# Scan and maxout kernel: two up-projections over weight differences, the third folded into the output product

## The chip, the cores and the metric

One Trainium2 chip, one core. The metric is the device time of one execution in microseconds, median of the timed runs.

## The reference

```python
# part one: a chunked state-space scan over x (4, 8, 768, 32), a, B, C -> y, same shape as x
# bridge: y becomes 3072 tokens of 256 values
x = np.ascontiguousarray(attn_out.transpose(0, 2, 1, 3)).reshape(B * S, H * D)
# part two: w1, w2, w3 are 256 x 768, w_out is 768 x 256
h = np.maximum(np.maximum(x @ w1, x @ w2), x @ w3)
return (h @ w_out).astype(np.float32)
```

All inputs and the output are float32.

## The kernel before

The 768 positions of the sequence are cut into six blocks (`c` = 0 to 5) of 128 positions. A block holds all four batches, so 512 tokens. For each block the scan gives `yT[c]`, the 256 values by 512 tokens, transposed. The feed-forward part then makes up-projections a, b, c with w1, w2, w3, their maximum `h`, and the output product with w_out. The scan of block n = c + 1 is woven into the feed-forward part of block c.

Block 0 is computed with plain products (`whole_group`, 512 columns each) while weights still arrive. Blocks 1 to 5 use a scheme that multiplies 2 x 2 blocks with seven products in place of eight. A slot `k` is one weight matrix (index i) for one pair of the six 128-column pieces of the hidden size (index q): seven products of 128 x 128 by 256 columns. Before, a block has nine slots, k = 3q + i.

A slot has two halves. `early` issues four products into the PSUM tiles sumA (one buffer) and sumB (two buffers), a ScalarE copy (L653) and three VectorE adds (L654 to L656). `late` issues the other three products, into parts of the same banks that the adds have read, then the first quarter of the maximum (L667, a copy, for i = 0; L669 otherwise) and one add of 512 (L670). It returns the maximum over the other three quarters (L673, 768 wide), which is put at the head of the list `later`. `pop(n)` runs the next n entries of `later`, so it decides where they stand in VectorE's queue.

The operands of the seven products are blocks of the weights and of y and sums of them. `weight_sums(k)` makes the four sums of a slot's weights on GpSimd (L613 to L616), two slots ahead of their use in block 1; they serve for all later blocks. `scan_sums` makes the four of y on VectorE (L553).

`down_next` issues half of the output product of one group of 128 tokens: three of six 128 x 128 by 256 products, into a bank from `ffn_bank`, which has one buffer by then. Four calls fill a bank, ScalarE copies it to SBUF and SP's queue stores it. The output products of block c run during block c + 1; those of block 5 come after everything else and are stored from ScalarE's queue.

The scan's steps that lie in the slots: `transposed` (trB and trC, L410), `scores` (L483: eight products over four banks from `att_bank`, which then has four buffers in rotation; the four products of scores and decay mask, L491 on VectorE, go to `later`), `scan_state` (L451, the sum into the state, `scan_sum`, goes to `later`), and "y" (`scan_old`, `scan_own`: L506 and L519, then `scan_y` and `scan_sums`). The masks come from DRAM; `decay_masks` (L384) clears the upper half on GpSimd and `part` does the exponentials on ScalarE (L391), four at a call. Block c + 2 is loaded on SP's queue in slot 0.

No scheduler reorders anything: each engine runs its instructions in the order in which the program issues them. That order is written by hand: for each slot the tables X, Y, P, D and K say which scan step or output product stands between `early` and `late` or behind `late`, and how many entries of `later` are run where. "E" below is `early`, "L" is `late`, "D" is `down_next`.

Of the kernel before, what the change touches and what calls it, by code (L numbers as in the profile page):

```python
# [19 lines left out]
def kernel(  # L20
# [398 lines left out]
    def scan_c(c):  # L419

        st = blocks[c]
        tr = st["trC"]
        st["CT"] = CT = att.tile([HN, NB, 2, P], FP32, tag="CT", name="CT")
        for g in range(2):
            nc.scalar.mul(CT[:, :, g], tr, parity[:, g:g + 1])
# [98 lines left out]
    def first_own(bs):  # L524
# [9 lines left out]
        if 0 not in yT:  # L534
            yT[0] = ffn.tile([P, KD, BLK], FP32, tag="yT", name="yT")
# [4 lines left out]
    def scan_y(c):  # L540
        yT[c] = ffn.tile([P, KD, BLK], FP32, tag="yT", name="yT")
        for t in range(KD):
            nc.scalar.copy(out=yT[c][:, t], in_=blocks[c]["y"][t].rearrange("p b i -> p (b i)"))
# [45 lines left out]
    NW = 3 * NQ  # L589
# [17 lines left out]
    def weight_sums(k):  # L607
        q, i = divmod(k, 3)
        a11, a12, a21, a22 = (
            w_sb[i][:, kk, (2 * q + g) * P:(2 * q + g + 1) * P]  # L610
# [7 lines left out]
    def left(p, k):  # L618
        if p in (1, 2, 4):
            q, i = divmod(k, 3)  # L620
            g, row = {1: (0, 0), 2: (0, 1), 4: (1, 1)}[p]
            f = 2 * q + g
            return w_sb[i][:, row, f * P:(f + 1) * P]
# [17 lines left out]
    def early(c, k):  # L641
        q, i = divmod(k, 3)
# [5 lines left out]
        if i > 0 and k % 2 not in quarters:  # L648
            quarters[k % 2] = kilos(HB)[:, 0:3]
        t = held["m"][:, 1:4] if i == 0 else quarters[k % 2]  # L650
# [8 lines left out]
    def late(c, k):  # L659
        q, i = divmod(k, 3)  # L660
# [3 lines left out]
        to = h_of(c)[:, 2 * q:2 * q + 2].rearrange(  # L664
            "p g (r t) -> p (g r) t", r=2) if i == 2 else m
        if i == 0:
            nc.scalar.copy(out=m[:, 0], in_=A[:, 0])  # L667
        else:
            nc.vector.tensor_tensor(out=to[:, 0], in0=m[:, 0], in1=A[:, 0], op=ALU.max)  # L669
        nc.vector.tensor_tensor(  # L670
            out=t[:, 0:2], in0=B, in1=eu[:, 1:2].to_broadcast([P, 2, HB]), op=ALU.add)
        if i > 0:
            return [lambda: nc.vector.tensor_tensor(  # L673
                out=to[:, 1:4], in0=m[:, 1:4], in1=t, op=ALU.max)]
        return []

    downs = []

    def down_next(kind=ffn_bank):
# [5 lines left out]
        last = c == NC - 1  # L685
        if j % (2 if last else 4) == 0:
# [3 lines left out]
        for f in range(half * NQ, (half + 1) * NQ):  # L690
            nc.tensor.matmul(  # L691
                out=o[:, i], lhsT=hT[c][:, f, b * P:(b + 1) * P], rhs=wo_sb[:, f],
                start=(f == 0), stop=(f == NF - 1), skip_group_check=True)
        if last and j % 2:
            ob = ffn.tile([P, 2, DM], FP32, tag="ob", bufs=3, name="ob")[:, 0]
            nc.scalar.copy(out=ob, in_=o[:, i])
            nc.scalar.dma_start(
                out=out.rearrange("(b s) m -> s b m", s=S)[c * P:(c + 1) * P, b], in_=ob)
        if not last and j % 4 == 3:
# [4 lines left out]
                in_=ob)  # L704

# [97 lines left out]
    for n in range(NF * 3):  # L803
# [58 lines left out]
        if n == 17:  # L862
# [15 lines left out]
    X1 = ["tc", "D", "D", "s0", "D", "s2", "A", "y", "D"]  # L878
    Y1 = ["", "", "D", "", "", "D", "", "D", "D"]
    P1 = [(1, 0, 0), (1, 0, 0), (1, 0, 1), (1, 4, 1), (1, 0, 0), (1, 1, 3), (1, 1, 0), (1, 0, 0),  # L880
          (9, 0, 0)]
    D1 = [(0, 0), (1, 0), (2, 0), (2, 0), (2, 0), (1, 0), (0, 2), (0, 1), (0, 2)]
    K1 = {0: (0, (0, 1)), 2: (0, (2, 3)), 4: (1, (0, 1)), 6: (1, (2, 3))}
    X2 = ["t", "s0", "D", "s2", "D", "y", "D", "D", "D"]
    Y2 = ["D", "D", "D", "", "", "", "", "", ""]
    P2 = [(1, 0, 1), (1, 2, 2), (1, 0, 0), (1, 4, 1), (1, 0, 0), (1, 0, 0), (9, 0, 0), (1, 0, 0),
          (1, 0, 0)]
    D2 = [(0, 0), (1, 0), (1, 0), (1, 0)] + 5 * [(0, 1)]
    K2 = {3: (1, (0, 1)), 5: (1, (2, 3))}
    X3, Y3, P3 = 8 * ["D"] + [""], 9 * [""], 9 * [(1, 0, 0)]  # L890

    for c in range(1, NC):
        n = c + 1
        xs, ys, ps_, ds, ks = (
            (X1, Y1, P1, D1, K1) if c == 1 else (X2, Y2, P2, D2, K2) if n < NC else
            (X3, Y3, P3, D2, {}))
        for k in range(NW):
            early(c, k)
            if c == 1 and k < 2:
                sign()  # L900
                if k == 0:
                    decode()
            part(n, ds[k][0])
            part(n + 1, ds[k][1])
            pop(ps_[k][0])
            x = xs[k]
            if x == "D":
                down_next()
            elif x == "A":
                later.append(scan_state(n, att_bank))  # L910
            elif x == "tc":
                scan_tc(n, att_bank)
            elif x == "t":
                transposed(n)
            elif x == "s0":
                scores(n, 0)
            elif x == "s2":
                scores(n, 2)
                if 1 < c < NC - 2:
                    later.insert(2, scan_state(n, ffn_bank))  # L920
            elif x == "y":
                scan_old(n)
                scan_own(n, range(NB))
                scan_y(n)
                scan_sums(n)
            pop(ps_[k][1])
            maximum = late(c, k)
            if c == 1 and k + 2 < NW:
                weight_sums(k + 2)
            if n < NC and k == 0:  # L930
# [47 lines left out]
```

## Time and profile before

| | |
|---|---|
| median of 3 timed runs | 296.35 us (296.31 to 296.82) |
| profiled execution, span from first to last instruction | 300.1 us |
| TensorE (PE) busy | 287.4 us, 96% |
| VectorE (DVE) busy | 199.9 us, 67% |
| ScalarE (ACT) busy | 121.1 us, 40% |
| GpSimd (POOL) busy | 72.1 us, 24% |
| start of blocks 1, 2, 3, 4, 5 in the span | 64.9, 113.2, 158.2, 203.2, 247.9 us |

The profiled execution has no time of its own beside the span. Matmuls are pipelined and their ends are modelled, so the price of one is read from the starts of a long row of them. A float32 matmul of this kernel shows as two records; a transpose as one.

### The profile page before, as it was taken

The page shows a single profiled execution, that of the slowest core. Times are in us where ns is not written, and L with a number is a line of the kernel's source. Part 1 is how long each engine was busy: PE and PEld are TensorE (multiplying, and loading weights), DVE is VectorE, ACT ScalarE, POOL GpSimd, SP SyncE. Part 2 cuts the span into 40 slices and gives each one's busy share as a digit, 9 for nine tenths or more (in the row PEclk, how much of TensorE's full clock was granted, in tenths as well). Part 3 has the DMA queues.
Part 4 walks back from the last instruction along what each step waited for, and adds up shares of the span by engine and source line. Part 5 has one row for each costly group of instructions (what it writes and reads, how often), then busy time and mean ns, then how long its engine had stood idle before and what let it go on. Part 6 is the DMA issues. An engine that isn't in the chain of part 4 may idle for free.

```text
span 300.1 us, 5303 instructions
## 1 busy us (share of the span) xinstructions
PE 287.4 (96%) x2024; PEld 225.1 (75%) x2024; DVE 199.9 (67%) x382; ACT 121.1 (40%) x315; POOL 72.1 (24%) x96
## 2 busy tenths in 40 slices
PE   6679999999999999999999999999999999999995
PEld 4557435477677788888888888888887888888784
DVE  2752867989588556867676867676867676667540
ACT  2934687943672545334344334344330211011200
POOL 5241647468991600007000006000000000000000
PEclk9957999999999999999999999999999999999999
DMA  7989879969969105792007790001010001010101
GB/s 88 189 274 290 214 140 175 223 173 183 177 141 127 35 2 167 186 131 46 2 0 207 162 136 22 3 2 35 0 37 0 2 0 35 2 36 0 35 20 52
DMA packets 105049, 28.13 MB, mean 94 GB/s; under 512 B 75328, under 2 KB 101952, under 8 KB 105024
## 3 DMA queue, kind: packets, MB, share of 16 engines
q1 hardware_dynamic: 104144, 27.14, 45.6%
q10 hardware_dynamic: 880, 0.66, 0.7%
q8 instruction: 16, 0.26, 0.4%
q14 instruction: 9, 0.07, 0.1%
HBM read 24.54 MB, written 3.24 MB: 93 GB/s over the span
## 4 chain that ended last, share of the span: by engine, by line
PE 81%; DVE 7%; POOL 3%; DMA 3%; SPq 2%; issue 2%; ACT 1%; POOLq 0%; DVEq 0%; ACTq 0%
PE sumB L628 25%; PE o L691 19%; PE sumA L628 18%; PE up L578 5%; PE s L483 4%; DMA raw_x<-in_x_dram 3%; PE y L519 3%; DVE L L491 2%; PE up L570 2%; PE y L506 1%; POOL w_u L185 1%; PE y L530 1%; SPq L125 1%; PE A L451 1%; SPq L159 1%
## 5 line engine op out<-in xcount | busy, mean ns | idle before, releaser
L691 PE MATMUL o<-wo,h 128*128 128x256 f32 x288 | 68.9, 379 | 0.0
L691 PEld LDWEIGHTS o<-wo,h 128*128 128x128 f32 x288 | 54.7, 190 | 7.4
L628 PE MATMUL sumA<-yT,w 128*128 128x256 f32 x180 | 55.5, 390 | 0.4 <-DVE eu L654 0.3
L391 ACT ACTIVATE L<-L,ncums 128x128 f32<-128x128 f32 x160 | 50.3, 391 | 8.9 <-POOL L L384 8.9
L653 ACT COPY eu<-sumA 128x256 f32<-128x256 f32 x45 | 16.7, 372 | 89.2 <-PE sumA L628 80.6
L628 PE MATMUL sumB<-rb 128*128 128x256 f32 x180 | 46.2, 379 | 0.0
L654 DVE TENSOR_TENSOR eu<-sumA,eu 128x256 f32<-128x256 f32 x45 | 19.0, 422 | 31.1 <-ACT eu L653 31.1
L628 PEld LDWEIGHTS sumA<-yT,w 128*128 128x128 f32 x180 | 31.9, 189 | 9.4 <-issue 2.5
L628 PEld LDWEIGHTS sumB<-rb 128*128 128x128 f32 x180 | 34.2, 190 | 4.6
L491 DVE TENSOR_TENSOR L<-s,L 128x512 f32<-128x512 f32 x46 | 29.3, 680 | 3.1 <-PE s L483 2.7
L578 PE MATMUL up<-yT,w 128*128 128x512 f32 x64 | 29.1, 600 | 0.2 <-DVE w L188 0.2
L628 PE MATMUL sumB<-yT,rb 128*128 128x256 f32 x90 | 27.6, 389 | 1.6 <-DVE rb L656 1.3
L670 DVE TENSOR_TENSOR rb<-sumB,eu 128x512 f32<-128x512 f32 x30 | 20.7, 689 | 10.9 <-PE sumB L628 10.8
L628 PE MATMUL sumA<-rb 128*128 128x256 f32 x90 | 26.9, 380 | 0.3 <-DVE rb L553 0.3
L628 PE MATMUL sumB<-rb,w 128*128 128x256 f32 x90 | 26.8, 379 | 0.0
L185 POOL TENSOR_TENSOR w_u<-w_u,w_r 128x512 uint32<-128x512 uint32 x12 | 15.3, 1272 | 32.6 <-DVE w_u L179 19.0
L578 PEld LDWEIGHTS up<-yT,w 128*128 128x128 f32 x64 | 11.6, 190 | 14.7 <-issue 11.6
L655 DVE TENSOR_TENSOR v<-sumB,eu 128x256 f32<-128x256 f32 x45 | 19.1, 425 | 4.7
L384 POOL TENSOR_SCALAR_AFFINE_SELECT L<-L 128x1024 f32<-128x1024 f32 x20 | 22.2, 1138 | 0.0
L628 PEld LDWEIGHTS sumB<-yT,rb 128*128 128x128 f32 x90 | 16.1, 189 | 7.0 <-DVE rb L656 2.1
L628 PEld LDWEIGHTS sumA<-rb 128*128 128x128 f32 x90 | 17.0, 190 | 2.9 <-POOL rb L613 0.7
L628 PEld LDWEIGHTS sumB<-rb,w 128*128 128x128 f32 x90 | 17.1, 190 | 2.3
(101 smaller groups left out, 324.0 us busy)
## 6 DMA issues: line engine op xcount, KB each, us to landing
L<-cums SPq DMA_DIRECT2D x10, 1024.0 KB, 8.8
rb<-in_moe_w_dram SPq DMA_DIRECT2D x9, 512.0 KB, 7.4
raw_x<-in_x_dram SPq DMA_DIRECT2D x6, 512.0 KB, 7.8
out_dram<-ob SPq DMA_DIRECT2D x10, 256.0 KB, 2.3
raw_B<-in_B_dram SPq DMA_DIRECT2D x6, 256.0 KB, 4.9
raw_C<-in_C_dram SPq DMA_DIRECT2D x6, 256.0 KB, 6.3
rb<-in_moe_w_out_dram SPq DMA_DIRECT2D x3, 512.0 KB, 6.3
E<-cums SPq DMA_DIRECT2D x40, 32.0 KB, 3.8
```

Of the source, the lines that this page charges most:

```text
L185: nc.gpsimd.tensor_tensor(out=u, in0=u, in1=r, op=ALU.add)
L384: nc.gpsimd.affine_select(out=Ls[c][:, b], in_=Ls[c][:, b], pattern=[[0, NH], [1, P]], compare_op=ALU.is_ge, fill=MASKED, base=0, channel_ ...
L391: nc.scalar.activation(L[:, b, h], L[:, b, h], AF.Exp, bias=ncum[c][:, b * NH + h:b * NH + h + 1], scale=1.0)
L483: nc.tensor.matmul(out=s[:, i].rearrange("j g i -> j (g i)"), lhsT=st["BT"][rows, b], rhs=st["CT"][rows, b].rearrange("p g i -> p (g i)"), ...
L491: nc.vector.tensor_tensor(out=M, in0=s, in1=M, op=ALU.mult)
L578: nc.tensor.matmul(out=bank, lhsT=w_sb[i][:, k, f * P:(f + 1) * P], rhs=yT[0][:, k], start=(k == 0), stop=(k == KD - 1))
L628: nc.tensor.matmul(out=bank[:, half], lhsT=left(p, k), rhs=sides[c][p], start=(first and half == 0), stop=True, skip_group_check=True)
L653: nc.scalar.copy(out=eu[:, 0], in_=A[:, 0])
L654: nc.vector.tensor_tensor(out=eu[:, 1], in0=A[:, 1], in1=eu[:, 0], op=ALU.add)
L655: nc.vector.tensor_tensor(out=v, in0=B[:, 1], in1=eu[:, 1], op=ALU.add)
L670: nc.vector.tensor_tensor(out=t[:, 0:2], in0=B, in1=eu[:, 1:2].to_broadcast([P, 2, HB]), op=ALU.add)
L691: nc.tensor.matmul(out=o[:, i], lhsT=hT[c][:, f, b * P:(b + 1) * P], rhs=wo_sb[:, f], start=(f == 0), stop=(f == NF - 1), skip_group_check ...
```

## The change

max(a, b, c) is written as b + max(a - b, c - b, 0). In blocks 1 to 5, VectorE first subtracts w2 from w1 and from w3 in place (L613 of the changed kernel, one piece of 512 in each `weight_sums`), and only the two differences are projected: six slots a block, k = 2q + i. `raised` takes the maximum of the two and zero in one instruction (scalar_tensor_tensor). b's part of the output is y w2 w_out. `turn_base` transposes w2 in block 1 (twelve 128 x 128 pieces), `fold_base` multiplies it with w_out into G (twelve products), and `terms` puts two products of y and G ahead of the six of h and w_out in each output group of blocks 1 to 5; half an output group is then four products. Block 0 stays as it was.

For that, yT has three buffers, and CT one. The plan of the slots is written anew as words (FIRST for block 1, STEADY for blocks 2 to 4, LAST for block 5): a digit n is pop(n), "x" and "z" are `part` of the next block and of the one after it, "m" and "n" are `decay_masks`, "g" is `turn_base`, "G3" three products of `fold_base`, "A" and "Af" are `scan_state`, and "l" is `last_next`, which issues two of the eight products of an output group of block 5, in banks of their own, as soon as their inputs are there.

```diff
--- before.py
+++ after.py
@@ -420,7 +420,7 @@
 
         st = blocks[c]
         tr = st["trC"]
-        st["CT"] = CT = att.tile([HN, NB, 2, P], FP32, tag="CT", name="CT")
+        st["CT"] = CT = att.tile([HN, NB, 2, P], FP32, tag="CT", bufs=1, name="CT")
         for g in range(2):
             nc.scalar.mul(CT[:, :, g], tr, parity[:, g:g + 1])
 
@@ -532,13 +532,13 @@
                     rhs=L0[:, b, h], start=(b % 2 == 0 and t == 0), stop=True,
                     tile_position=(0, q * D), skip_group_check=True)
         if 0 not in yT:
-            yT[0] = ffn.tile([P, KD, BLK], FP32, tag="yT", name="yT")
+            yT[0] = ffn.tile([P, KD, BLK], FP32, tag="yT", bufs=3, name="yT")
         r = bs[0] // 2
         nc.scalar.copy(
             out=yT[0][:, :, r * HB:(r + 1) * HB], in_=y.rearrange("p t b i -> p t (b i)"))
 
     def scan_y(c):
-        yT[c] = ffn.tile([P, KD, BLK], FP32, tag="yT", name="yT")
+        yT[c] = ffn.tile([P, KD, BLK], FP32, tag="yT", bufs=3, name="yT")
         for t in range(KD):
             nc.scalar.copy(out=yT[c][:, t], in_=blocks[c]["y"][t].rearrange("p b i -> p (b i)"))
 
@@ -586,7 +586,9 @@
 
 
 
-    NW = 3 * NQ
+    DIFF = (0, 2)
+    BASE = 1
+    NW = len(DIFF) * NQ
     ysum, wsum = [], {}
 
     def kilos(b):
@@ -605,9 +607,13 @@
         ysum.extend(kilos(HB) for _ in range(2))
 
     def weight_sums(k):
-        q, i = divmod(k, 3)
+        q, i = divmod(k, 2)
+        w = w_sb[DIFF[i]]
+        cols = slice(2 * q * P, 2 * (q + 1) * P)
+        nc.vector.tensor_tensor(
+            out=w[:, :, cols], in0=w[:, :, cols], in1=w_sb[BASE][:, :, cols], op=ALU.subtract)
         a11, a12, a21, a22 = (
-            w_sb[i][:, kk, (2 * q + g) * P:(2 * q + g + 1) * P]
+            w[:, kk, (2 * q + g) * P:(2 * q + g + 1) * P]
             for g in range(2) for kk in range(2))
         s1, s2, s3, s4 = (wsum[k][:, j] for j in range(4))
         nc.gpsimd.tensor_tensor(out=s1, in0=a21, in1=a22, op=ALU.add)
@@ -617,10 +623,10 @@
 
     def left(p, k):
         if p in (1, 2, 4):
-            q, i = divmod(k, 3)
+            q, i = divmod(k, 2)
             g, row = {1: (0, 0), 2: (0, 1), 4: (1, 1)}[p]
             f = 2 * q + g
-            return w_sb[i][:, row, f * P:(f + 1) * P]
+            return w_sb[DIFF[i]][:, row, f * P:(f + 1) * P]
         return wsum[k][:, {5: 0, 6: 1, 7: 2, 3: 3}[p]]
 
     def products(c, k, which, first):
...
@@ -657,24 +663,67 @@
         held["open"] = A, B, eu, t
 
     def late(c, k):
-        q, i = divmod(k, 3)
+        q, i = divmod(k, 2)
         m = held["m"]
         A, B, eu, t = held.pop("open")
         products(c, k, [(2, A, 0), (3, B, 0), (4, B, 1)], False)
-        to = h_of(c)[:, 2 * q:2 * q + 2].rearrange(
-            "p g (r t) -> p (g r) t", r=2) if i == 2 else m
         if i == 0:
             nc.scalar.copy(out=m[:, 0], in_=A[:, 0])
+            to = m
         else:
-            nc.vector.tensor_tensor(out=to[:, 0], in0=m[:, 0], in1=A[:, 0], op=ALU.max)
+            to = h_of(c)[:, 2 * q:2 * q + 2].rearrange("p g (r t) -> p (g r) t", r=2)
+            raised(to[:, 0], m[:, 0], A[:, 0])
         nc.vector.tensor_tensor(
             out=t[:, 0:2], in0=B, in1=eu[:, 1:2].to_broadcast([P, 2, HB]), op=ALU.add)
         if i > 0:
-            return [lambda: nc.vector.tensor_tensor(
-                out=to[:, 1:4], in0=m[:, 1:4], in1=t, op=ALU.max)]
+            return [lambda: raised(to[:, 1:4], m[:, 1:4], t)]
         return []
 
+    def raised(out, one, two):
+
+        nc.vector.scalar_tensor_tensor(
+            out=out, in0=one, scalar=0.0, in1=two, op0=ALU.max, op1=ALU.max)
+
+    based = {}
+
+    def turn_base(q):
+
+        if "T" not in based:
+            one, two = kilos(DM), kilos(DM)
+            based["T"] = [one[:, f] for f in range(4)] + [two[:, f] for f in range(NF - 4)]
+            based["pairs"] = [one[:, 0:2], one[:, 2:4], two[:, 0:2]]
+            based["G"] = two[:, NF - 4:NF - 4 + KD]
+        tp = att_bank([P, 2, DM], "w2T_tp")
+        for g in range(2):
+            f = 2 * q + g
+            for k in range(KD):
+                nc.tensor.transpose(
+                    out=tp[:, g, k * P:(k + 1) * P], in_=w_sb[BASE][:, k, f * P:(f + 1) * P],
+                    identity=ident)
+        two = based["pairs"][q]
+        nc.scalar.copy(out=two, in_=tp)
+
+    def fold_base(n):
+
+        if "sum" not in based:
+            based["sum"] = att_bank([P, KD, DM], "fold")
+            based["steps"] = [(k, f) for k in range(KD) for f in range(NF)]
+        for _ in range(n):
+            k, f = based["steps"].pop(0)
+            nc.tensor.matmul(
+                out=based["sum"][:, k], lhsT=based["T"][f][:, k * P:(k + 1) * P], rhs=wo_sb[:, f],
+                start=(f == 0), stop=(f == NF - 1), skip_group_check=True)
+        if not based["steps"]:
+            nc.scalar.copy(out=based["G"], in_=based["sum"])
+
     downs = []
+
+    def terms(c):
+
+        up = [(hT[c][:, f], wo_sb[:, f]) for f in range(NF)]
+        if c == 0:
+            return up
+        return [(yT[c][:, k], based["G"][:, k]) for k in range(KD)] + up
 
     def down_next(kind=ffn_bank):
 
@@ -682,26 +731,42 @@
             return
         c, j = downs.pop(0)
         u, i, half = j // 4, j // 2 % 2, j % 2
-        last = c == NC - 1
-        if j % (2 if last else 4) == 0:
+        if j % 4 == 0:
             held["o"] = kind([P, 2, DM], "o")
         o = held["o"]
         b = 2 * u + i
-        for f in range(half * NQ, (half + 1) * NQ):
+        all_terms = terms(c)
+        n = len(all_terms) // 2
+        for z, (left_, right_) in list(enumerate(all_terms))[half * n:(half + 1) * n]:
             nc.tensor.matmul(
-                out=o[:, i], lhsT=hT[c][:, f, b * P:(b + 1) * P], rhs=wo_sb[:, f],
-                start=(f == 0), stop=(f == NF - 1), skip_group_check=True)
...
+                out=o[:, i], lhsT=left_[:, b * P:(b + 1) * P], rhs=right_,
+                start=(z == 0), stop=(z == 2 * n - 1), skip_group_check=True)
+        if j % 4 == 3:
             ob = ffn.tile([P, 2, DM], FP32, tag="ob", bufs=3, name="ob")
             nc.scalar.copy(out=ob, in_=o)
             nc.sync.dma_start(
                 out=out.rearrange("(b s) m -> s b m", s=S)[c * P:(c + 1) * P, 2 * u:2 * u + 2],
                 in_=ob)
+
+    last = []
+
+    def last_next():
+
+        c = NC - 1
+        if "last" not in held:
+            held["last"] = [att_bank([P, 2, DM], "o") for _ in range(2)]
+        b, piece = last.pop(0)
+        o = held["last"][b // 2]
+        for z in (2 * piece, 2 * piece + 1):
+            left_, right_ = terms(c)[z]
+            nc.tensor.matmul(
+                out=o[:, b % 2], lhsT=left_[:, b * P:(b + 1) * P], rhs=right_,
+                start=(z == 0 and b % 2 == 0), stop=True, skip_group_check=True)
+        if piece == 3:
+            ob = ffn.tile([P, 2, DM], FP32, tag="ob", bufs=3, name="ob")[:, 0]
+            nc.scalar.copy(out=ob, in_=o[:, b % 2])
+            nc.scalar.dma_start(
+                out=out.rearrange("(b s) m -> s b m", s=S)[c * P:(c + 1) * P, b], in_=ob)
 
 
     for b in range(2, NB):
@@ -875,76 +940,96 @@
 
 
 
...
+    FIRST = [
+        "E tc g L load c e g m01",
+        "E 1 x2 D L D m23",
+        "E 1 x2 s0 L 2 D g",
+        "E 2 x2 D L s2 n01",
+        "E 1 x2 2 D L 2 A D z2 G3 n23",
+        "E 1 y G3 4 L 1 z1 D G3 z1 D G3 z1",
+    ]
+    STEADY = [
+        "E 1 x1 t D L load c e D",
+        "E 1 x1 D L s0",
+        "E 1 2 x1 D L 2 s2 Af 3 n01",
+        "E 2 z1 D L",
+        "E 1 y 4 z1 L D n23 z1",
+        "E z2 D L D",
+    ]
+    LAST = [
+        "E 1 D L D",
+        "E D L",
+        "E 1 D L D l",
+        "E l D L l",
+        "E 1 l D L l",
+        "E D L 1 l l l",
+    ]
+
+    def act(c, word):
+        n = c + 1
+        if word.isdigit():
+            pop(int(word))
+        elif word == "D":
+            down_next()
+        elif word == "l":
+            last_next()
+        elif word == "tc":
+            scan_tc(n, att_bank)
+        elif word == "t":
+            transposed(n)
+        elif word == "c":
+            scan_c(n)
+        elif word == "e":
+            scan_e(n)
+            later.append(lambda: scan_cd(n))
+        elif word == "load":
+            loads(c + 2)
+        elif word in ("s0", "s2"):
+            scores(n, int(word[1]))
+        elif word in ("A", "Af"):
+            if n < NC - 1:
+                step = scan_state(n, ffn_bank if word == "Af" else att_bank)
+                later.insert(min(2, len(later)), step)
+        elif word == "y":
+            scan_old(n)
+            scan_own(n, range(NB))
+            scan_y(n)
+            scan_sums(n)
+        elif word == "g":
+            turn_base(based.setdefault("turned", 0))
+            based["turned"] += 1
+        elif word[0] == "G":
+            fold_base(int(word[1]))
+        elif word[0] in "xz":
+            part(n + (word[0] == "z"), int(word[1]))
+        elif word[0] in "mn":
+            m = n + (word[0] == "n")
+            if m < NC:
+                decay_masks(m, [int(d) for d in word[1:]])
 
     for c in range(1, NC):
...
+        plan = FIRST if c == 1 else STEADY if c < NC - 1 else LAST
+        if c == NC - 1:
+            last += [(b, p) for p in range(2) for b in range(NB)]
+            last += [(b, 2) for b in range(NB)] + [(b, 3) for b in range(NB)]
         for k in range(NW):
...
+            for word in plan[k].split():
+                if word == "E":
+                    early(c, k)
+                    if c == 1 and k < 2:
+                        sign()
+                        if k == 0:
+                            decode()
+                elif word == "L":
+                    later[:0] = late(c, k)
+                    if c == 1 and k + 2 < NW:
+                        weight_sums(k + 2)
+                else:
+                    act(c, word)
+        if c < NC - 1:
+            downs += [(c, j) for j in range(8)]
+    while last:
+        last_next()
 
 
 # ---- launch: one core; inputs and outputs as the reference has them ----
```

More of the change, by code (lines that the diff above doesn't have):

```diff
@@ L646, in early @@
             held["m"] = ffn.tile([P, 4, HB], FP32, tag="m", name="m")
-        if i > 0 and k % 2 not in quarters:
-            quarters[k % 2] = kilos(HB)[:, 0:3]
-        t = held["m"][:, 1:4] if i == 0 else quarters[k % 2]
+        if i > 0 and q % 2 not in quarters:
+            quarters[q % 2] = kilos(HB)[:, 0:3]
+        t = held["m"][:, 1:4] if i == 0 else quarters[q % 2]
         eu = wtmp.tile([P, 2, HB], FP32, tag="w_u", name="eu")
@@ L659, in late @@
     def late(c, k):
-        q, i = divmod(k, 3)
+        q, i = divmod(k, 2)
         m = held["m"]
@@ L689, in down_next @@
         b = 2 * u + i
-        for f in range(half * NQ, (half + 1) * NQ):
+        all_terms = terms(c)
+        n = len(all_terms) // 2
+        for z, (left_, right_) in list(enumerate(all_terms))[half * n:(half + 1) * n]:
             nc.tensor.matmul(
-                out=o[:, i], lhsT=hT[c][:, f, b * P:(b + 1) * P], rhs=wo_sb[:, f],
-                start=(f == 0), stop=(f == NF - 1), skip_group_check=True)
[L694 to L699, printed above, removed]
+                out=o[:, i], lhsT=left_[:, b * P:(b + 1) * P], rhs=right_,
+                start=(z == 0), stop=(z == 2 * n - 1), skip_group_check=True)
+        if j % 4 == 3:
             ob = ffn.tile([P, 2, DM], FP32, tag="ob", bufs=3, name="ob")
@@ L873 @@
     downs += [(0, j) for j in range(8)]
[L878 to L890, printed above, removed]
+    FIRST = [
[6 more added lines that the diff above has]
+    ]
@@ L892 @@
     for c in range(1, NC):
[L893 to L896, printed above, removed]
+        plan = FIRST if c == 1 else STEADY if c < NC - 1 else LAST
+        if c == NC - 1:
+            last += [(b, p) for p in range(2) for b in range(NB)]
+            last += [(b, 2) for b in range(NB)] + [(b, 3) for b in range(NB)]
         for k in range(NW):
[L898 to L930, printed above, removed]
-                loads(c + 2)
-            if n < NC and k == 0:
-                scan_c(n)
-            if n < NC and k == 2 * int(c == 1):
-                scan_e(n)
-                later.append(lambda: scan_cd(n))
-            pop(ps_[k][2])
-            later[:0] = maximum
-            if ys[k] == "D":
-                down_next()
-            if k in ks and n + ks[k][0] < NC:
-                decay_masks(n + ks[k][0], ks[k][1])
@@ L943 @@
-        if n == NC:
-            pop(9)
-        downs += [(c, j) for j in range(8)]
-    while downs:
-        down_next(att_bank)
+            for word in plan[k].split():
[11 more added lines that the diff above has]
+                    act(c, word)
```

## The prediction

> **What bounds the kernel now.** I read the page's busy time and slices first, then busy time per block, then the costliest groups, then the timeline of one slot.
>
> ```profile
> PE 287.4 (96%) x2024; PEld 225.1 (75%) x2024; DVE 199.9 (67%) x382; ACT 121.1 (40%) x315; POOL 72.1 (24%) x96
> ...
> PE   6679999999999999999999999999999999999995
> ...
> PEclk9957999999999999999999999999999999999999
> ```
>
> TensorE is busy from slice 4 to the end at full granted clock. Whether busy means bound is read per block: blocks 1 to 5, cut at the first up-projection of each.
>
> ```profile
> 64.90:113.15 48.25, 46.66 (x340) 36.60 (x339) 35.18 (x70) 24.46 (x74) 30.56 (x48) 1.00 0.62 111
> 113.15:158.20 45.05, 45.05 (x343) 37.97 (x343) 31.92 (x62) 19.05 (x53) 6.59 (x7) 1.00 0.47 89
> 158.20:203.21 45.01, 45.01 (x344) 37.93 (x343) 32.06 (x62) 18.47 (x52) 5.53 (x6) 1.00 0.46 89
> 203.21:247.86 44.65, 44.41 (x312) 37.37 (x311) 31.64 (x61) 12.49 (x32) 0.00 (x0) 1.00 0.04 12
> 247.86:300.10 52.24, 48.61 (x223) 41.71 (x222) 26.77 (x50) 7.03 (x18) 0.00 (x0) 0.99 0.08 26
> ```
>
> Columns: stretch, length, busy PE, weight loads, DVE, ACT, POOL, clock, DMA share, GB/s. In blocks 2 and 3 PE has no idle time at all, DVE fills 71%: here a matmul taken out shortens the block by its whole price, as long as the other engines' answers still come in time.
>
> ```profile
> L691 PE MATMUL o<-wo,h 128*128 128x256 f32 x288 | 68.9, 379 | 0.0
> ...
> L628 PE MATMUL sumA<-yT,w 128*128 128x256 f32 x180 | 55.5, 390 | 0.4 <-DVE eu L654 0.3
> ...
> L491 DVE TENSOR_TENSOR L<-s,L 128x512 f32<-128x512 f32 x46 | 29.3, 680 | 3.1 <-PE s L483 2.7
> ```
>
> A matmul of 256 columns shows as two records (288 for 144 products), and means overlap, so the price comes from the chain: 48 records of the last output products take 10.37 us, 0.432 us for a matmul.
>
> ```profile
> 124.08 0.59 PE L628 MATMUL sumA<-yT,w 128*128 128x256 f32 x2
> ...
> 125.20 0.37 ACT L653 COPY eu<-sumA 128x256 f32<-128x256 f32 x1 [4.04 <-PE sumA L628]
> ...
> 125.61 0.42 DVE L654 TENSOR_TENSOR eu<-sumA,eu 128x256 f32<-128x256 f32 x1 [0.65 <-ACT eu L653]
> ...
> 126.14 0.42 DVE L655 TENSOR_TENSOR v<-sumB,eu 128x256 f32<-128x256 f32 x1
> ...
> 126.59 0.42 DVE L656 TENSOR_TENSOR rb<-sumB,v 128x256 f32<-128x256 f32 x1
> ...
> 126.94 0.95 DVE L673 TENSOR_TENSOR m<-m,rb 128x768 f32<-128x768 f32 x1
> ```
>
> This is one slot's answer: from the start E of its first product, the third add ends at E+2.93 and a 768 maximum popped behind it at E+3.81. The second product of `late` waits for the third add; PE covers that with 1.73 of `early` and whatever is put between.
>
> **The change, part by part.** Times are made against the profiled execution, span 300.1; the page gives no other time of it. The median of the timed runs is 296.35, 3.75 less; I carry the difference over.
>
> Removed on PE: per block 1 to 5, three of nine slots, 21 matmuls; added, 8 matmuls y times G in the outputs of that block (four 128-token groups, two halves of y). Net 13 x 5 = 65 matmuls, 65 x 0.432 = -28.1 us. The built order shows these counts (six groups of seven, output products of eight terms).
>
> Added on PE in block 1: 12 fold products, 12 x 0.432 = +5.2; 12 transposes: `trB` of four takes 0.43 to its successor in the timeline (114.98 to 115.42), 12 x 0.11 = +1.3. The Trainium skill (TensorE: Matmul & The Clock Gate, Part 4: PE-mode transpose) gives some 275 ns for one in a kernel; estimated from it the transposes are 3.3 and the sum 2.0 worse. The trace shows a mean of 277 for one record, but 0.11 from start to start, so the overlap is what page and row differ by.
>
> DVE: each slot removed takes off 0.42+0.42+0.42+0.69 and, for two of three, a 256 and a 768 maximum. `raised` runs as SCALAR_TENSOR_TENSOR; the only such rows (L188, 512 wide) go from 0.68, the price of a plain 512, to a mean of 0.90. I take the plain price, 0.95 for 768; the far end is 1.25. DVE falls to some 23 of about 41 us a steady block, so it doesn't become the bound as a whole.
>
> DVE, the six weight differences: 512 wide, both inputs in SBUF, 0.68 each by L491. Four lie in block 1 behind `late`'s add, hidden by an output product of 1.30, except where a bank is awaited (below). Two lie at the end of block 0, where DVE is busy 10.22 of 11.00 us (55 to 66 us): one ahead of the last mask products, one right ahead of the four L553 differences, the last of which ended at 66.1 while product 6 waited at 65.8. Bounds 0 and 1.4; I take 0.6, the second one less its slack.
>
> ACT gains four 512 copies (0.59 each by L701) in block 1, for the transposed pairs and the fold, and loses three 256 copies a block; it is busy 24.46 of 48.25. POOL loses three of the nine rounds of four sums, about 2.1 us each, and has no new work. The order of SP's queue is unchanged: loads of block c+2 in slot 0, issued from 114.5 to 131.5 in block 2, fit a block of 41 us. CT with one buffer: its last reader is some 20 us before its next writer (without that, its two copies on ACT, 1.27, would stand ahead of the scores). Three yT buffers only keep y for the output a block later. All at nothing, with that cover.
>
> **The new wait.** In the plan for blocks 2 to 4, slot 2 runs "E 1 2 x1 D L 2 s2": the second score group stands right behind the pops that free two of its four banks. Bank by bank: s0 took four banks in slot 1; two of its products are popped before `late`, two after it. The built order shows a DVE wait on each of the first four score matmuls here; before, that group had none. PE: 1.73 + 1.73 (D is now four matmuls) + 1.30 = E+4.76, where scores want to start. DVE: third add E+2.93, 768 maximum E+3.81, two L491 (1.28 as a pair) E+5.0, then the 512 add of `late`, done about E+5.6, and two more L491, E+6.9. The fourth bank is free then; one plus four score matmuls at 0.135 follow, E+7.6, against E+5.9 without a wait. Behind it on PE stands everything. 1.7 x 3 blocks = +5.1. Bounds: nothing, if the banks were free; 2.6 a block, if the 768 takes its far end and the products run late.
>
> Block 1's own waits: it idles 48.25 - 46.66 = 1.6 now, mostly in its first slots. New is the third transpose pair, which wants the bank of the first mask product: after `late` PE has one output product, 1.30, while DVE has 0.69 + 0.68 + 0.68 behind an add that starts 0.16 late: about 1.0. Against that, slots 0 and 1 have more PE work between `early` and `late`: net -0.5, between -1.5 and +2.
>
> Block 4's stall (0.4, at 227.8) and the last block's uncovered last slot (0.27 + 0.56, at 284.4 and 285.4) go: every slot has an output product inside, and 22 output matmuls (9.5 us) follow the last `late`. -1.2. The four last stores now follow 0.86 us apart instead of 2.59; copy and issue are 0.37 + 0.38 on ACT, so they keep up: +0.2, end after PE 3.2 as before.
>
> Sum: -28.1 + 5.2 + 1.3 + 0.6 + 5.1 - 0.5 - 1.2 + 0.2 = -17.4. 300.1 becomes 282.7, the median 296.35 becomes 279.0.
>
> **The rivals.** *The scores don't wait.* If DVE is ahead or the banks come otherwise, the 5.1 goes: 273.9. Against it: the waits in the built order. Chance 0.14.
>
> *Differences and POOL hold each other up.* This line shows a 768 maximum between 0.946 and 1.289:
>
> ```profile
> L673 DVE TENSOR_TENSOR h<-m,rb x15: 946/948/1289, 83.6 to 287.3; 128x768 f32<-128x768 f32 x15
> ```
>
> The longest fell at 83.6 while POOL did weight sums, one of which, at 78.6, took 1.18 instead of 0.45. A difference could wait for a whole mask step (1.14), and each leads a round of POOL sums that its slot needs two slots on. Four of six on the path: +4.6, 283.6; with the sums late as well, up to 286. For it, POOL's 63% in block 1; against it, a spare slot for every round. Chance 0.18. The Trainium skill (SBUF: State Buffer, Who interferes with whom) states this as a lock: a VectorE instruction with two SBUF inputs and a GpSimd one that reads SBUF exclude each other for the whole instruction. It speaks against the differences; the stretched rows agree with it.
>
> *The answer chain becomes the bound.* Where a slot had nothing between `early` and `late` (the last one before) PE lost 0.83. If all 30 remaining slots lost that, 24.9 more: 303.9, slower. It decides from 17.4 / 30 = 0.58 a slot. For it: DVE's chain per slot is as long as ever, and the work that covers it was laid out anew. Against it: every slot has 1.3 us or more inside, and 1.73 + 1.30 covers the 2.93. Chance 0.03. *The saving is eaten exactly*, or the change doesn't do what it says: the order shows the products gone, so 0.01, at 296.
>
> **How the numbers follow.** The forecast, 279.0, has 0.64. Its own bounds, with waits in the scores from 1.0 to 2.3 and block 1's ends, are 276 to 283. The range 273.5 to 286 takes in the first two rivals and leaves out some 0.1. About 0.2% is what a measurement of this kernel can tell from no change. Faster 0.96, same 0.01, slower 0.03.
>
> **What would show it.** PE records of L634 at 420 instead of 630, and 0.432 a matmul kept. Blocks 2 and 3 at 41.1 us with 1.7 idle, all in slot 2 ahead of the scores, released by DVE L491; block 1 at about 45; the last block near 46 to PE's end. Steady blocks of 39.4 would prove the first rival; more than 2 us idle in block 1 with DVE's differences or POOL's sums as releasers the second; waits on the third add in most slots the third. An added matmul that takes longer than 0.432 would make the sum wrong at its root.

## The result and the profile after

The kernel after takes 283.16 us (median), the kernel before in the same comparison 296.59. The ratio is 0.955, interval 0.953 to 0.957. The gain is 13.4 us; 17.4 was forecast. 283.2 lies inside the range, 4.2 above the forecast of 279.0.

Some executions of either kernel, the profiled one of before among them, run TensorE at half clock for 10.24 us inside block 0 and take some 5 us longer, and the ratios and ranges of times below leave them out. So 300.1 is no partner for the span after, 281.2. In both kernels a run's time is 1.7 us above its span (282.91 against 281.2), which puts the span of before at 294.6 without that stretch. Its blocks 1 to 5 are not touched (235.2 us together), so its block 0 would be 59.4; this figure is worked out, not profiled.

The page after, its busy times and slices:

```profile
PE 267.4 (95%) x1930; PEld 209.6 (75%) x1930; DVE 159.0 (57%) x298; ACT 116.6 (41%) x304; POOL 67.2 (24%) x84
...
PE   6889999989989999999999999999999999999994
...
PEclk9999999999999999997999999999999999999999
```

TensorE is as full as before, and VectorE fell from 67% to 57%, so the bound stayed where it was. New is the 7 in the clock row: a stretch at half clock in slice 19, in block 2.

Busy time per block (stretch, length, PE, weight loads, DVE, ACT, POOL, clock, DMA share, GB/s), blocks 1 to 5:

```profile
59.88:106.12 46.24, 43.16 (x335) 34.94 (x333) 31.70 (x58) 24.20 (x71) 26.61 (x36) 1.00 0.65 124
106.12:148.85 42.73, 42.16 (x318) 35.05 (x317) 22.06 (x43) 18.04 (x53) 6.58 (x7) 0.96 0.50 94
148.85:190.00 41.15, 40.58 (x317) 34.01 (x316) 22.83 (x44) 17.01 (x49) 5.52 (x6) 1.00 0.52 97
190.00:230.58 40.58, 40.01 (x286) 33.52 (x285) 22.50 (x43) 11.07 (x29) 0.00 (x0) 1.00 0.04 14
230.58:281.20 50.62, 46.45 (x213) 39.92 (x211) 16.61 (x31) 6.50 (x16) 0.00 (x0) 1.00 0.08 27
```

Set against the forecast, block by block (before, after, change, forecast change):

| block | before | after | change | forecast | missing |
|---|---|---|---|---|---|
| 0 | 59.4 | 59.9 | +0.5 | +0.6 | -0.1 |
| 1 | 48.25 | 46.24 | -2.0 | -3.1 | 1.1 |
| 2 | 45.05 | 42.73 | -2.3 | -3.9 | 1.6 |
| 3 | 45.01 | 41.15 | -3.9 | -3.9 | 0.0 |
| 4 | 44.65 | 40.58 | -4.1 | -4.3 | 0.2 |
| 5 | 52.24 | 50.62 | -1.6 | -2.8 | 1.2 |

The forecasts are sums of the prediction's own terms: in block 1, 21 products go (-9.1), folds and transposes come (+6.5), waits -0.5; in blocks 2 and 3, 13 net products (-5.6) and a wait of 1.7; block 4 the same and its stall; in block 5, 5 net products (-2.2), -0.8 and +0.2. The missing 4 us sit in blocks 1, 2 and 5.

The costliest groups that answer to those of before:

```profile
L741 PE MATMUL o<-wo,h 128*128 128x256 f32 x240 | 58.4, 379 | 0.0
L634 PE MATMUL sumA<-yT,w 128*128 128x256 f32 x120 | 37.5, 394 | 0.0
...
L491 DVE TENSOR_TENSOR L<-s,L 128x512 f32<-128x512 f32 x46 | 29.3, 681 | 2.9 <-PE s L483 2.9
L684 DVE SCALAR_TENSOR_TENSOR h<-m,rb 128x768 f32<-128x768 f32 x15 | 14.7, 981 | 0.1
```

The same instructions at nearly the same mean, and of the products fewer. The maximum of three in one instruction (L684) takes 0.98 on the mean for 768 columns, close to the plain price of 0.95 that was taken.

TensorE's waits (who waited, for whom: us in total, times, longest):

```profile
PE s L483 <- DVE L L491: 1.7, 3, 0.6
...
PE sumA L634 <- POOL rb L619: 1.3, 1, 1.3
PE o L762 <- ACT ob L767: 0.9, 2, 0.5
PE w2T_tp L700 <- DVE L L491: 0.9, 1, 0.9
```

The first row was forecast by place and releaser, the last by size (about 1.0). The two in the middle were not forecast. The last column is the longest single wait. Slot 2 of block 3 shows the first of them:

```profile
161.04 1.15 PE L483 MATMUL s<-CT,BT 32*128 32x256 f32 x16
...
162.12 0.70 PE L634 MATMUL sumA<-yT,w 128*128 128x256 f32 x2
...
165.07 0.95 DVE L684 SCALAR_TENSOR_TENSOR h<-m,rb 128x768 f32<-128x768 f32 x1
...
165.94 1.28 DVE L491 TENSOR_TENSOR L<-s,L 128x512 f32<-128x512 f32 x2
...
167.06 0.97 PE L483 MATMUL s<-CT,BT 32*128 32x256 f32 x4
167.17 0.69 DVE L676 TENSOR_TENSOR m<-sumB,eu 128x512 f32<-128x512 f32 x1
167.78 1.28 DVE L491 TENSOR_TENSOR L<-s,L 128x512 f32<-128x512 f32 x2
168.61 1.69 PE L483 MATMUL s<-CT,BT 32*128 32x256 f32 x12 [0.57 <-DVE L L491]
...
170.23 0.65 PE L451 MATMUL A<-raw_x,Bd 128*32 128x64 f32 x32
```

With E = 162.12: the scores start at E+4.94 (forecast E+4.76) and DVE's last mask product ends at 169.06, E+6.94 (forecast E+6.9). Only 0.57 shows as idle time; the rest of the wait is inside the two score rows, because a stretched group counts as busy. The first score group, in slot 1, goes from first score to next product in 162.12 - 161.04 = 1.08; here that takes 170.23 - 167.06 = 3.17. The wait is 2.1 us at its place, not 0.57: read the starts, not the idle column.

### The profile page after: what moved, and what is told of

It reads as the page before. It is cut to its first block, busy times and chain, and to the rows that moved or that the text cites. A ratio compares the mean times of both kernels' runs of the same rounds, so it can differ in the third digit from the quotient of the medians.

```text
span 281.2 us, 4990 instructions
## 1 busy us (share of the span) xinstructions
PE 267.4 (95%) x1930; PEld 209.6 (75%) x1930; DVE 159.0 (57%) x298; ACT 116.6 (41%) x304; POOL 67.2 (24%) x84
## 4 chain that ended last, share of the span: by engine, by line
PE 80%; DVE 13%; POOL 2%; ACT 2%; issue 2%; POOLq 0%; DVEq 0%; ACTq 0%
PE o L741 21%; PE sumB L634 16%; PE sumA L634 14%; PE up L578 6%; PE o L762 5%; PE s L483 5%; DVE L L491 4%; PE y L519 3%; PE fold L713 2%; PE y L506 1%; PE up L570 1%; PE spread L320 1%; DVE m L676 1%; DVE w_u L176 1%; DVE w L613 1%
## 5 line engine op out<-in xcount | busy, mean ns | idle before, releaser
L741 PE MATMUL o<-wo,h 128*128 128x256 f32 x240 | 58.4, 379 | 0.0
L634 PE MATMUL sumA<-yT,w 128*128 128x256 f32 x120 | 37.5, 394 | 0.0
L634 PE MATMUL sumB<-rb 128*128 128x256 f32 x120 | 30.8, 379 | 0.0
L634 PEld LDWEIGHTS sumA<-yT,w 128*128 128x128 f32 x120 | 21.7, 192 | 5.5 <-issue 1.4
L634 PEld LDWEIGHTS sumB<-rb 128*128 128x128 f32 x120 | 23.0, 192 | 3.2
L483 PE MATMUL s<-CT,BT 32*128 32x256 f32 x192 | 19.6, 403 | 3.1 <-DVE L L491 1.7
L634 PE MATMUL sumA<-rb 128*128 128x256 f32 x60 | 18.4, 389 | 1.3 <-POOL rb L619 1.3
L483 PEld LDWEIGHTS s<-CT,BT 32*128 32x128 f32 x192 | 12.1, 184 | 10.0 <-issue 6.4
L634 PE MATMUL sumB<-yT,rb 128*128 128x256 f32 x60 | 18.1, 383 | 0.7 <-POOL rb L621 0.4
L634 PE MATMUL sumB<-rb,w 128*128 128x256 f32 x60 | 17.8, 379 | 0.0
L741 PE MATMUL o<-rb,yT 128*128 128x256 f32 x64 | 16.4, 379 | 0.0
L676 DVE TENSOR_TENSOR m<-sumB,eu 128x512 f32<-128x512 f32 x15 | 10.3, 688 | 10.6 <-PE sumB L634 10.5
```

Of the source, the lines that this page charges most:

```text
L483: nc.tensor.matmul(out=s[:, i].rearrange("j g i -> j (g i)"), lhsT=st["BT"][rows, b], rhs=st["CT"][rows, b].rearrange("p g i -> p (g i)"), ...
L634: nc.tensor.matmul(out=bank[:, half], lhsT=left(p, k), rhs=sides[c][p], start=(first and half == 0), stop=True, skip_group_check=True)
L676: nc.vector.tensor_tensor(out=t[:, 0:2], in0=B, in1=eu[:, 1:2].to_broadcast([P, 2, HB]), op=ALU.add)
L741: nc.tensor.matmul(out=o[:, i], lhsT=left_[:, b * P:(b + 1) * P], rhs=right_, start=(z == 0), stop=(z == 2 * n - 1), skip_group_check=True)
```

## The experiments

**The kernel before, again** (no edit).

> The kernel before, profiled once more. Its first profile had TensorE at half the granted clock for 10.24 us in block 0. If that dip alone makes the 3.75 us between its span and the median, a profile without it has a span near 294.6, block 1 starts near 59.3 in place of 64.9, and blocks 1 to 5 keep 48.2, 45.0, 45.0, 44.6 and 52.2 us. If instead the dip hid something else, the blocks behind it differ too.

One run: 301.4, span 299.7, mean clock 0.982, again with the 10.24 us of half clock in block 0; blocks 1 to 5 as long as in the first profile. So no profile of before without that stretch was had. With the timed runs of 296.3 to 296.8 it says that the first profile's extra 5 us were its execution's, and not the kernel's.

**The kernel after, again** (no edit).

> The changed kernel once more, for a second profile. Theory (the half clock of 3.4 us in block 2 comes from how the wait in slot 2 falls against the clock's windows, so it is there in some executions and not in others): undisturbed executions fall near 281.5 without it and near 283 with it. Rival (the wait always brings it): all near 283.

282.2 to 285.0 us, ratio 0.957 (0.952 to 0.961). In its profile block 2 is 41.16, although the scores wait there as before; the half clock stands at block 1's start, right behind a wait:

```profile
62.69 1.22 PE L634 MATMUL sumA<-rb 128*128 128x256 f32 x2 [2.17 <-POOL rb L621]
63.70 1.91 PE L634 MATMUL sumB<-rb 128*128 128x256 f32 x4
```

Two records in 1.22 in place of 0.60. So block 2's missing 1.6 belongs to an execution: a half-clock stretch of 3.41 us costs half its length, and comes in one place or another, or not at all (one of the four runs was 282.16 at a mean clock of 1.0). The theory's 281.5 for that case was 0.7 too low.

**The second score group a slot later.** The first plan moves the scores, the state's sum and the popped mask products:

```diff
-        "E 1 2 x1 D L 2 s2 Af 3 n01",
-        "E 2 z1 D L",
-        "E 1 y 4 z1 L D n23 z1",
+        "E 1 2 x1 D L 2 Af 1 n01",
+        "E s2 z1 D 2 L 1",
+        "E 2 D y 4 z1 L n23 z1",
```

> The changed kernel with the second score group moved from the end of slot 2 into slot 3 in blocks 2 to 4, behind early, when all four banks are free. Theory (bank wait, and the half clock of block 2 follows from it): 1.7 to 1.9 us less in each of three blocks and the 1.6 of the dip in block 2, so 283.2 becomes about 276.3; blocks 2 to 4 near 39.3 us each, clock 1.00 from block 1 on. Rival (the dip belongs to the place in the run, not to the wait): 5.4 less, about 277.8, with a dip of 3.4 us somewhere in blocks 2 to 5. Rival (the scores do not hold PE up, they only stand where DVE is late anyway): the wait moves to the next matmul and the time stays within 1 us of 283.2.

278.0 to 280.4 us, ratio 0.942 (0.938 to 0.947); 276.3 was expected. Blocks 2 and 3 are 40.44 (first products at 111.09, 151.53 and 191.97): the scores no longer wait, but slot 5 starts 0.91 late in each, released by the ScalarE copy `m` (L671), which stood behind the exponentials "z1" of slot 4.

```profile
PE sumA L634 <- ACT m L671: 1.8, 2, 0.9
```

The second plan puts them behind `late`:

```diff
-        "E 2 D y 4 z1 L n23 z1",
+        "E 2 D y 4 L z1 n23 z1",
```

> As the run with the second score group in slot 3, with the first mask exponentials of slot 4 moved behind late, so that ScalarE copies the first quarter of the maximum before them. Theory (the bank wait is worth 1.7 to 1.9 a block, and 0.9 of it had come back as a wait for that copy): blocks 2 to 4 near 39.4 in place of 40.4, 3 us under the earlier run, 275.1 without any half clock. Rival (scores in slot 3 cost PE as much as they saved): no gain over 278.0.

276.0 to 278.3 us, ratio 0.934 (0.931 to 0.938). Blocks 2 and 3:

```profile
108.16:147.59 39.43, 39.43 (x317) 32.93 (x316) 22.56 (x43) 17.96 (x53) 6.58 (x7) 1.00 0.56 102
147.59:187.02 39.43, 39.43 (x318) 32.94 (x316) 22.79 (x44) 16.90 (x49) 5.52 (x6) 1.00 0.52 101
```

PE has no idle time, and 39.43 is the 39.4 that the prediction names for scores that don't wait. By blocks the wait is worth 41.15 - 39.43 = 1.72, three times over. (It is 2.1 at its place; the new order gives some of that back, such as 0.10 ahead of the state's products, and not all of the 0.4 was traced.) The lowest times of the two plans are 2.0 apart, not 3: the copy had held up blocks 2 and 3, and not block 4, which has no "z1" to run.

**The last stores in alternating order.** The last pieces of two batches write into the two halves of one bank; b = 0, 1, 2, 3 becomes 0, 2, 1, 3.

```diff
-            last += [(b, 2) for b in range(NB)] + [(b, 3) for b in range(NB)]
+            last += [(b, 2) for b in range(NB)] + [(b, 3) for b in (0, 2, 1, 3)]
```

> The changed kernel with the last four pieces of the outputs of block 5 in the order 0, 2, 1, 3 in place of 0, 1, 2, 3, so that neighbours lie in different banks. Theory (a piece waits for the ScalarE copy out of the same bank): two waits of 0.46 and the refill behind each go, 1.0 to 1.1 less, about 282.1. Rival (the end is set by the stores, not by the pieces): no change, 283.2.

279.3 to 282.0 us, ratio 0.947 (0.942 to 0.952). TensorE at the end of the kernel after:

```profile
266.84 7.07 PE L762 MATMUL o<-wo,h 128*128 128x256 f32 x32
274.37 1.99 PE L762 MATMUL o<-wo,h 128*128 128x256 f32 x8 [0.46 <-ACT ob L767]
276.83 1.13 PE L762 MATMUL o<-wo,h 128*128 128x256 f32 x4 [0.47 <-ACT ob L767]
```

and in alternating order:

```profile
265.29 9.66 PE L762 MATMUL o<-wo,h 128*128 128x256 f32 x44
```

44 records take 277.96 - 266.84 = 11.12 in the one and 9.66 in the other. A product into the second half of a bank waited for the ScalarE copy out of the first half; with the other bank between, it doesn't. That is 1.46 of the last block, where 1.0 to 1.1 was expected.

**The weight differences.** Three kernels: without them (the second operands of the up-projections are then w1 and w3 themselves), with all six on GpSimd, and, on the best version below, with the first two on GpSimd.

```diff
-        nc.vector.tensor_tensor(
-            out=w[:, :, cols], in0=w[:, :, cols], in1=w_sb[BASE][:, :, cols], op=ALU.subtract)
```

> The changed kernel without the six weight differences on DVE (the sums are then made of w1 and w3 themselves, so this part of the computation is left out). Theory (the differences cost the start of block 1 and, through the lock with POOL, some of its first slots): 1.5 to 2.5 less, about 281.2, block 1 near 44.5 us. Rival (they are hidden as forecast but for 0.6): 282.6. Rival (block 1 is slow for the transposes and folds): no change within 0.3.

278.8 us, ratio 0.942 (0.939 to 0.945). Block 0 ends at 59.36 in place of 59.88, and block 1 takes 43.93:

```profile
59.36:103.29 43.93, 42.92 (x334) 35.03 (x333) 27.66 (x53) 24.35 (x71) 24.77 (x36) 1.00 0.72 134
```

So the differences cost 0.5 in block 0 and 2.3 in block 1. The wait in the first slot is gone, and the third transpose pair waits 0.3 in place of 0.9. The rest of the 4.4 us between 283.2 and 278.8 is the half-clock stretch, which no execution of this kernel had (mean clock 0.999 to 1.0).

```diff
-        nc.vector.tensor_tensor(
+        nc.gpsimd.tensor_tensor(
```

> The changed kernel with the six weight differences on GpSimd in place of DVE. Theory (a difference on DVE takes 1.1 in place of 0.68 because it waits for a running GpSimd step, and stands ahead of DVE's adds): without it DVE answers sooner, block 1 falls from 46.2 to about 44.5, 281.5 in all. Rival (GpSimd is the late one in block 1): its rounds of sums come 1.2 later each, slots wait for them, 284 or more.

282.0 us, ratio 0.952 (0.950 to 0.954); block 1:

```profile
59.16:105.50 46.34, 43.25 (x334) 34.95 (x333) 27.49 (x53) 24.34 (x71) 32.22 (x41) 1.00 0.68 129
```

Not shorter, where 44.5 was expected: POOL goes from 26.6 to 32.2 us, the wait at the first slot's second product is gone, and others take its place in slots 1 and 2 (1.06 and 0.48 at the longest).

```diff
-        nc.vector.tensor_tensor(
+        (nc.gpsimd if k < 2 else nc.vector).tensor_tensor(
```

> As the run before, and the first two of the six weight differences (those at the end of block 0) on GpSimd in place of VectorE. Theory (these two on VectorE are what delays product 6 of block 1's first slot, and the other four are hidden): the wait of 1.3 to 2.8 at product 6 goes and block 1 is as short as without differences, 43.9 or less; 273.5 to 274.2. Rival (all six share in it, or GpSimd's longer rounds come late): the wait stays, or slots 1 and 2 wait for the sums; 275 to 276 as without the change.

Ratio 0.926 (0.923 to 0.930), against 0.928 (0.926 to 0.930) without this edit: the chip doesn't tell the two apart. The first slot's wait is gone, as the theory said, but block 1 is 46.36 against 46.38, where 43.9 was expected. The waits that it shows instead:

```profile
PE sumA L634 <- DVE eu L660: 1.2, 1, 1.2
PE w2T_tp L700 <- DVE L L491: 1.1, 1, 1.1
```

In its timeline the first of these goes back to ScalarE, whose copy `eu` stood behind exponentials that had waited for GpSimd's masks. The work on six blocks of weights has to be somewhere in block 1; moved to GpSimd it delays the masks, left on VectorE the sums of y and the mask products.

**No fold.** Transposes, fold products and their copies are left out, w_out standing in for G.

```diff
-        return [(yT[c][:, k], based["G"][:, k]) for k in range(KD)] + up
+        return [(yT[c][:, k], wo_sb[:, k]) for k in range(KD)] + up
...
-        "E tc g L load c e g m01",
+        "E tc L load c e m01",
...
-        "E 1 x2 s0 L 2 D g",
+        "E 1 x2 s0 L 2 D",
...
-        "E 1 x2 2 D L 2 A D z2 G3 n23",
-        "E 1 y G3 4 L 1 z1 D G3 z1 D G3 z1",
+        "E 1 x2 2 D L 2 A D z2 n23",
+        "E 1 y 4 L 1 z1 D z1 D z1",
```

> The twelve transposes of w2, the twelve fold products and their four ScalarE copies in block 1 are left out; two blocks of w_out stand in place of G in the output products (this part of the computation is changed). Theory (each is paid at its plain price on TensorE): 12 x 0.432 + 12 x 0.11 = 6.5, and the wait of the third transpose pair (0.86) goes with them, so block 1 is 7.4 shorter (about 39 in a profile) and the time 275.8 against 283.2. Rival (they also covered waits of block 1's answers): block 1 falls by 4 to 5 only and shows new waits on the third add or on the sums; 278 to 279. In both the wait at product 6 of block 1's first slot stays.

275.2 to 276.6 us, ratio 0.930 (0.928 to 0.933). Block 1 is 40.04, 6.2 shorter and not 7.4:

```profile
60.09:100.13 40.04, 36.46 (x299) 29.32 (x298) 32.39 (x58) 22.38 (x67) 26.71 (x36) 1.00 0.80 156
```

It has a new wait of 2.00 on the sum `eu`, behind a ScalarE activation that waited 3.41 for the transfer of E:

```profile
PE sumA L634 <- DVE eu L660: 2.0, 1, 2.0
```

Without each kernel's long waits, block 1 is 46.24 - 1.35 - 0.86 = 44.03 with the fold and 40.04 - 0.74 - 2.00 = 37.30 without: the fold's own price is 6.7, where 6.5 was forecast. Both theories had a part: the plain price is right, and the fold also covered a transfer.

**No y times G.** The added products of blocks 1 to 4 are left out (32 of them).

```diff
-        if c == 0:
+        if c < NC - 1:
             return up
```

> The changed kernel without the products of y and G in the outputs of blocks 1 to 4 (this part of the computation is left out): 32 matmuls fewer, and the output product inside a slot is back at three matmuls, 1.30 us. Theory (PE bound, 0.432 a matmul, 1.73 + 1.30 still covers the third add at 2.93): 13.8 less, about 269.3 where the changed kernel has 283.2, less up to 1 us given back in the waits for the scores, which then start 0.4 earlier. Rival (the answer chain is the bound below four matmuls): waits on the third add in most slots and under 9 us gained.

271.2 to 275.1 us, ratio 0.921 (0.914 to 0.928). The two lower times, 271.2 and 271.9, are 11 to 12 below the kernel after; the profiled execution, 275.1, has three half-clock stretches. 32 x 0.432 = 13.8, less the scores' wait, which grows by the missing product (0.43 in each of three blocks): 12.5. Blocks 2 and 3 were 39.96 and 39.92 with a half-clock stretch in each; no slot waits for its third add beyond 0.2. So with one product less as cover in every slot the answer chain still is not the bound.

**The two improvements together** (scores a slot later with the exponentials behind, and alternating last stores).

> The plan of the scores a slot later with its masks behind (e5) and the last stores in alternating order (e2) together. Theory (the two gains stand in different blocks and add): e5 gave 276.0 in executions without a half-clock stretch and 276.9 as the median; alternating stores save 0.9 to 1.1 in the last block: 275.0 without such a stretch, 276 as the median. Rival (the end is set by the stores' transfers, so the last pieces' gain is lost): 276.0 and 276.9 again.

274.3 to 275.8 us, ratio 0.928 (0.926 to 0.930). This beats both kernels.

```profile
106.48:145.92 39.44, 39.44 (x318) 32.93 (x317) 22.58 (x43) 17.98 (x53) 6.59 (x7) 1.00 0.54 102
145.92:185.35 39.43, 39.43 (x317) 32.93 (x316) 22.78 (x44) 16.92 (x49) 5.54 (x6) 1.00 0.52 101
185.35:224.22 38.87, 38.87 (x285) 32.87 (x284) 22.45 (x43) 11.08 (x29) 0.00 (x0) 1.00 0.04 15
224.22:273.40 49.18, 45.92 (x213) 40.09 (x211) 16.61 (x31) 6.50 (x16) 0.00 (x0) 1.00 0.08 27
```

Blocks 2 to 4 have no idle time on PE, and block 5 is 1.44 shorter than 50.62. The two gains add: 1.72 + 1.72 + 1.71 + 1.44 = 6.6, and the time goes from 282.2, the one execution of after at a mean clock of 1.0, to 274.3 to 275.8.

## Why the prediction was right and wrong

**The price of a product, right.** 0.432 kept in after: 32 records of the last pieces in 7.07 (31 gaps of 0.216 and one record of 0.38). The records of L634 number 420 (120 + 120 + 60 + 60 + 60). Block 3 was forecast at 41.1 and is 41.15.

**The scores' wait, right.** Place, releaser and size: 1.72 by blocks for a forecast of 1.7. Two marks of its working hold too (E+4.94, E+6.94). The third does not: the products behind the scores start at E+8.11, not E+7.6, so the wait is 2.1 at its place, and that the block agrees to 0.02 is in part luck. The sign, 1.7 idle, showed as 0.57, for the reason given above. The first rival, scores that don't wait, fell; moving them gave the time it named for a steady block.

**The fold and its transposes, right.** 6.7 for 6.5. The price from the starts (0.11 a transpose) held. By the estimate from the Trainium skill (TensorE: Matmul & The Clock Gate, Part 4: PE-mode transpose) the sum would have been 8.5; the measurement decides for 6.5. (The page's figure stands beside one for bf16; here the data are float32.)

**Block 0's differences and block 4, right**: +0.5 for +0.6 (block 0 is also 0.5 shorter in the kernel without differences), and -4.1 for -4.3.

**Block 1's own waits, mis-sized by 1.1.** The term was -0.5; it measures -2.0 + 9.07 - 6.5 = +0.6. The third transpose pair waited 0.86, as forecast. Most of what failed is the price of the differences and their place:

```profile
59.41 0.69 DVE L613 TENSOR_TENSOR w<-w,w 128x512 f32<-128x512 f32 x1
...
59.64 1.58 POOL L185 TENSOR_TENSOR w_u<-w_u,w_r 128x512 uint32<-128x512 uint32 x1 [3.29 <-DVE w_u L179]
...
60.54 0.42 DVE L553 TENSOR_TENSOR rb<-y,rb 128x256 f32<-128x256 f32 x1
...
61.82 0.70 PE L634 MATMUL sumA<-rb 128*128 128x256 f32 x2 [1.35 <-POOL rb L619]
```

In the kernel with the first two differences on GpSimd, the same place:

```profile
59.96 0.60 PE L634 MATMUL sumA<-yT,w 128*128 128x256 f32 x2
60.09 0.43 DVE L553 TENSOR_TENSOR rb<-y,rb 128x256 f32<-128x256 f32 x1
...
60.66 0.67 PE L634 MATMUL sumA<-rb 128*128 128x256 f32 x2
```

The second product of the first slot needs the second sum of y (L553), and the difference stands ahead of it on VectorE. The prediction saw this (it took "the second one less its slack") and put the price into block 0; the wait falls behind the first product, in block 1, so both carry it. The releaser that the row names, L619, is no cause: it belongs to slot 1's sums, and in the kernel without fold the product starts before that instruction ends. Of the 1.35, 0.74 is the wait for the sum of y, as the kernel without fold shows it (before had 0.27 there); the other 0.6 is not explained by the difference (see the last section). In slot 1 a difference of 1.45 stands ahead of the adds, and the third of them is then waited for 0.38. And the six differences took 0.68 to 1.50, a mean of 1.09, not 0.68.

**The second rival, half right.** It said that differences and GpSimd would stretch each other: three of six took 1.45 to 1.50, and the GpSimd instruction beside the short one above took 1.58 in place of 1.27. The trace agrees with what the Trainium skill (SBUF: State Buffer, Who interferes with whom) states as a lock. Its size did not come: it asked 4.6 on the path beyond the forecast, and leaving the differences out gains 2.8 in all (0.5 + 2.3), where the sum had 0.6 for block 0 and about 1.0 for the third transpose pair. The 2.8 holds the unexplained 0.6 too.

**The last stores, mis-sized by 1.2.** The term "+0.2: they keep up" compared copy and issue (0.37 + 0.38) with the 0.86 between stores. It left out that TensorE waits for the copy as well, since both halves of a bank share it: 1.46 by the reordering.

**Block 2, 1.6 not in the sum.** A half-clock stretch of 3.41 us behind the scores' wait. The second profile of the same kernel has it in block 1 and none in block 2, so it is no fixed part of the wait's price; but by the mean clock seven of the eight executions of after had one somewhere. The prediction put it at nothing: the profile of before shows no such stretch behind block 0. The last section shows when it came.

**The third rival** (answer chain, slower) is not seen: no row of after waits for a third add beyond 0.4, and the run without y times G, with less cover, neither.

## What to carry to other kernels

When products are removed from a bound engine, price them from starts in a long row, then spend the effort on what the removal brings together: banks whose readers were far away, and one-off work placed at a seam where a queue is already full. Here the plain prices were right to 0.2. What was missed was a half-clock stretch (1.6), the start of block 1 (1.1), and the order in which the last outputs fill the two halves of a bank (1.2). A wait can hide in rows that count as busy, so measure it between starts, or by the length of a block with and without it.

## What the runs showed of the hardware that was not expected

Half-clock stretches come in lengths of 3.41 us and 10.24 us (three times that). The seven short ones in the profiles begin between 0.24 us before the end of a wait of TensorE and 2.4 us behind it (behind the scores' wait in block 2 in the first profile of after, at the 2.17 in the second). A wait doesn't decide it alone: with alternating stores a wait of 2.84 at block 1's start was followed by none.

The traces also record when the granted clock changes. In all profiles the time between two changes is a whole multiple of 3.413 us (in after 119.47, 35 times, then 3.41, then 150.19, 44 times), so the changes lie on a grid, and what tells the cases apart is how much of a wait falls into one cell of it. At block 1's first slot, idle times of 1.93, 2.02 and 2.24 us in one cell were followed by a half-clock cell; 1.35 and 1.46 were not, and neither was the 2.84, which the grid cuts into 1.43 and 1.41. Of the 21 score groups that wait, in seven profiles, four have 2.66 to 3.17 us from first score to next product in one cell, and these four were followed by a half-clock cell; the other 17 have at most 2.48 and were not. In after that is block 2 (2.91) against blocks 3 and 4 (2.03 and 2.22). This is a pattern read from the traces; no run shifted a wait against the grid. The Trainium skill (TensorE: Matmul & The Clock Gate, Part 1) has a gate that judges activity in a window of 4096 cycles, 3413 ns, and says that it is free-running. The length and the grid agree. That half rate takes an idle time of at least a whole window does not: the waits here were shorter than 3.4 us. What kind of activity inside a window counts, no run here shows.

The wait at block 1's first slot is longer than the difference explains (0.25 after the second L553 ends in the kernel without fold, 0.86 in after). It may be TensorE waiting for its own instructions. The DMA queues of after:

```profile
q8 instruction: 15, 0.25, 0.4%
```

Its 15 packets and TensorE's 2 x 1930 matmuls and weight loads make 257 instructions for a packet; before, 16 packets and 2 x 2024 make 253. In six profiles of the kernel after and its variants, the third packet starts at 59.4, 59.6, 60.0, 60.4, 60.6 and 60.6 and the second product of the first slot at 61.8, 62.2, 62.7, 62.8, 63.1 and 63.2, each 2.4 to 2.7 later. In the four where it starts at 54.8 to 56.7 there is no wait, or only the 0.74 for the sum of y. In the first plan of the scores, with block 1 starting late at 64.89, it starts at 62.5 and the product at 66.4, 0.4 after the end of its sum of y. The DMA engines are full up to there (a share of 1.16 from 58 to 60 us). That loads delay the packet, and the packet the product, is argued from these starts only; no run moved the loads.
